# Which slots of an interleaved attention and MoE kernel run the first projection, in which PSUM bank, and which engine rectifies it

## The chip, the cores and the metric

The kernel runs on one core of a Trainium2 chip. The metric is the device time of one execution in microseconds. The engines are TensorE (PE in the profile, PEld for its weight loads), VectorE (DVE), ScalarE (ACT), GpSimd (POOL) and SyncE (SP, which here only issues DMAs).

## The reference

```python
# q, k, v: (8, 8, 576, 64) float32; w_in: (512, 2048); w_out: (2048, 512); tau = 0.02
scores = scale * np.matmul(q, k.transpose(0, 1, 3, 2))
thresh = np.max(scores, axis=-1, keepdims=True) - tau
scores = np.where(scores >= thresh, scores, -1000000000.0)
attn = np.exp(scores - np.max(scores, axis=-1, keepdims=True))
attn = attn / (np.sum(attn, axis=-1, keepdims=True) + 1e-09)
x = np.matmul(attn, v)             # heads side by side: (4608, 512)
h = x @ w_in
out = (h * np.clip(h + 3.0, 0.0, 6.0) / 6.0) @ w_out
```

So 64 heads of thresholded attention over 576 positions are followed by a two-layer MLP with a gated activation (the MoE part, with one expert). Below, "first projection" is the product with `w_in` and "second projection" the product with `w_out`.

## The kernel before

**Slots.** The order of all instructions is written out by hand; each engine runs its own instructions in that order and waits on semaphores. The work is cut into 144 slots, numbered n. A quad is four heads (two pairs) and takes nine slots: four for each pair, of 128 query rows of both heads, and one, slot 8 of the quad, for the last 64 rows of all four. Two quads make one batch element, so the order repeats with a period of 18 slots. I write c = n mod 18 for the place in the period.

**What one slot does, in the order of issue (the main loop, from L477).**

1. ScalarE: exponentials of the slot before with their sums (`sm_exp`, L309).
2. VectorE: two copies of the scores out of PSUM with row maxima (`sm_max`, L296); GpSimd makes a bias of each (L299).
3. One item of the first projection, if there is one to do: eight matmuls on TensorE (`mm1`, L372), a rectifier (`mm1_relu`: `r = max(h + 3, 0)`, on ScalarE at L380 or on VectorE at L382) and a gate on VectorE (`mm1_gate`, L387: `min(r, 6) * h`). In slots with an attention product the gate is put behind that product's copies.
4. VectorE: reciprocal of the sums of the slot before (`sm_recip`, L312).
5. In even slots only: up to two parts of the second projection (`mm2_part`, L397, four matmuls each; four parts make one output tile), and after a fourth part the output copy (`mm2_out`, L405 on VectorE), whose DMA is issued a slot later (L418).
6. ScalarE: masks (`sm_mask`, L304), which wait for the bias.
7. The slot's planned jobs: transposes of k on TensorE (L217, the 64 last rows L238) with a copy on ScalarE (L207), transposes of q (on VectorE, L226, from the third batch element on), attention products with v on TensorE (L341, L344) with copies on VectorE to `xT` (L352) and for the last rows to `xR` (L362).
8. After odd slots: scores of the two next slots on TensorE (L269, L275 for slot 8 of a quad). The scores of a slot need its PSUM region free, so the copies with maxima of the slot two before must have run.
9. GpSimd: normalisation of the slot before (`sm_norm`, L317); SP issues its DMA transposition (L325). GpSimd also issues the loads of v (L125, L129; one each in four slots of a period, c = 9 to 12) and at the start those of the weights (L146, L150).

From n = 22 (N1) on, attention products and transposes use PSUM banks 5 and 2, which the scores of even slots also use.

**Items.** The attention product at c = 3 (`av1`, with the rest `avr`) completes a batch element and puts 16 items into `todo1`. They run one a slot from c = 4 on. After the 8th and the 16th, eight parts of the second projection each go into `todo2`. Four batch elements' last rows make eight more items, `todo3`, which are there from n = 75 on and run only where `todo1` is empty. Attention products stand at c = 3, 9, 13 and 17.

**Banks.** A first projection accumulates in bank HB = 6; in odd slots it takes bank OB = 7, which is the second projection's, when `todo2` is empty:

```python
if todo1 or todo3:
    item, then = (todo1 or todo3).pop(0)
    h = mm1(item, hb=HB if n % 2 == 0 or todo2 else OB)
    r = mm1_relu(h, on_act=n % 2 == 0)
```

A projection can start in a bank only when the gate (or the output copy) that read the bank's last content is done.

Of the kernel before, what the change touches and what calls it, by code (L numbers as in the profile page):

```python
# [21 lines left out]
def kernel(  # L22
# [18 lines left out]
    NSLOT = 9  # L41
    NB = 2
    N1 = 22
    HB = 6
    OB = 7
# [74 lines left out]
    def load_v(b):  # L120
        vm = v_pool.tile([P, H, 4 * D], BF16, tag="vm", name="vm")
        vr = vrs[b % 2]
        vsb[b] = (vm, vr)
        for g in range(2):
            vcasts.append(lambda g=g: nc.gpsimd.dma_start(  # L125
                out=vm[:, g * 4:g * 4 + 4, :],
                in_=v[b, g * 4:g * 4 + 4, 0:512, :].rearrange("h (p t) d -> p h (t d)", t=4)))
        for a in range(2):
            vcasts.append(lambda a=a: nc.gpsimd.dma_start(  # L129
                out=vr[a * 64:(a + 1) * 64, a, :, :],  # L130
                in_=v[b, :, 512:S, :].rearrange("(hp a) p d -> a p hp d", a=2)[a]))
# [49 lines left out]
    def alloc_qk(quad):  # L181
        qkT[quad] = (qk_pool.tile([P, 2, S], F32, tag="qT", name="qT"),
                     qk_pool.tile([P, 2, S + 64], F32, tag="kT", name="kT"))
# [105 lines left out]
    def sm_max(sl):  # L289
        sl.s = s_pool.tile([P, 2, S], F32, tag="s", name="s")  # L290
        sl.m = stat_pool.tile([P, 2], F32, tag="m", name="m")
        sl.bias = stat_pool.tile([P, 2], F32, tag="bias", name="bias")
        sl.rsum = stat_pool.tile([P, 2], F32, tag="rsum", name="rsum")
        sl.rinv = stat_pool.tile([P, 2], F32, tag="rinv", name="rinv")
        for i in range(2):
            nc.vector.tensor_scalar(out=sl.s[:, i, :], in0=score_tile(sl.n, i),  # L296
                                    scalar1=1.0, scalar2=None, op0=Alu.mult, op1=Alu.max,
                                    accum_out=sl.m[:, i:i + 1])
            nc.gpsimd.tensor_scalar(out=sl.bias[:, i:i + 1], in0=sl.m[:, i:i + 1], scalar1=-scale, scalar2=tau,  # L299
                                    op0=Alu.mult, op1=Alu.add)  # L300

    def sm_mask(sl, i):
        s = sl.s[:, i, :]
        nc.scalar.activation(out=s, in_=s, func=Act.Prelu, bias=sl.bias[:, i:i + 1], scale=scale,  # L304
                             alpha=REJECT)

    def sm_exp(sl, i):
        s = sl.s[:, i, :]
        nc.scalar.activation(out=s, in_=s, func=Act.Exp, accum_out=sl.rsum[:, i:i + 1])  # L309

    def sm_recip(sl):
        nc.vector.reciprocal(out=sl.rinv[:], in_=sl.rsum[:])  # L312
# [15 lines left out]
    def pe_transpose(sl):  # L328
        pb = ps_flat[:, 3072:3072 + S].bitcast(BF16).rearrange("p (c t) -> p c t", t=P)
        pn = sl.pn[:].rearrange("p a b -> p (a b)")  # L330
        for c in range(9):
            nc.tensor.transpose(pb[:, c, :], pn[:, c * P:(c + 1) * P], identb[:])
        return lambda: nc.vector.tensor_copy(out=sl.dst, in_=pb)
# [33 lines left out]
    def mm1(item, hb=HB):  # L367
        src, ni, c0, _ = item
        hps = ps[:, hb, :].rearrange("p (n w) -> p n w", n=2)
        for n in range(2):  # L370
            for ki in range(KI):
                nc.tensor.matmul(hps[:, n, :], w_in_sb[:, ki, (ni + n) * P:(ni + n + 1) * P],  # L372
                                 src[:, ki, c0:c0 + 256], start=(ki == 0), stop=(ki == KI - 1))
        return hps


    def mm1_relu(hps, on_act):
        r = r_pool.tile([P, 2, 256], F32, tag="r", name="r")[:]
        if on_act:
            nc.scalar.activation(out=r, in_=hps, func=Act.Relu, bias=three[:])  # L380
        else:
            nc.vector.tensor_scalar(out=r, in0=hps, scalar1=3.0, scalar2=0.0, op0=Alu.add, op1=Alu.max)  # L382
        return r

    def mm1_gate(item, hps, r):
        _, ni, _, g0 = item
        nc.vector.scalar_tensor_tensor(out=gbuf[:, ni:ni + 2, g0:g0 + 256], in0=r, scalar=6.0, in1=hps,  # L387
                                       op0=Alu.min, op1=Alu.mult)
# [3 lines left out]
    def mm2_part(b, t, part, ob=OB):  # L392
        g0 = M + 64 * (3 - b % 4) if t == 4 else 512 * (b % 2) + P * t
        if part == 0:
            o_ps[0] = ps[:, ob, :]
        for ni in range(part * 4, part * 4 + 4):
            nc.tensor.matmul(o_ps[0], gbuf[:, ni, g0:g0 + P], w_out_sb[:, ni, :],  # L397
                             start=(ni == 0), stop=(ni == NI - 1))
# [12 lines left out]
    todo1 = []  # L411
    todo3 = []
    todo2 = []
# [63 lines left out]
    for n, sl in enumerate(queue):  # L477
        quad, slot = sl.quad, sl.slot
        b, g = divmod(quad, 2)
        now = n  # L480
        if slot in (0, 4):
            pts[2 * quad + slot // 4] = pt_pool.tile([P, 9, 512], BF16, tag="pT", name="pT")
        if slot == 8:
            ptr[quad] = ptr_pool.tile([P, 9, P], BF16, tag="pR", name="pR")
        if quad == 0 and slot == 0:
            load_quad(1)
        if slot == (4 if quad else 8) and quad + 2 < NQUAD:
            load_quad(quad + 2)
        if slot == 0 and g == 1 and b + 1 < B:
            load_v(b + 1)  # L490
        if prev is not None:
            for i in range(2):
                sm_exp(prev, i)
        sm_max(sl)

        gate = None
        if todo1 or todo3:
            item, then = (todo1 or todo3).pop(0)
            h = mm1(item, hb=HB if n % 2 == 0 or todo2 else OB)
            r = mm1_relu(h, on_act=n % 2 == 0)  # L500
            gate = lambda item=item, h=h, r=r: mm1_gate(item, h, r)
            if not any(job[:2] == "av" for job in plan[n]):
                gate()
                gate = None
            late2 = then
        else:
            late2 = ()
        copies = pe_transpose(queue[n - 2]) if n > 1 and queue[n - 2].on_chip else None
        if prev is not None:
            sm_recip(prev)  # L510
        if copies:
            copies()
        outs = []


        for _ in range(0 if n % 2 else 2):
            if todo2:
                b2, t2, part = todo2.pop(0)
                mm2_part(b2, t2, part)
                if part == 3:  # L520
                    outs += mm2_out(b2, t2, on_act=False)
        for i in range(2):
            sm_mask(sl, i)
        nxt = 2 * quad + 2
        for job in plan[n]:
            if gate and job[:2] != "av":
                gate()
                gate = None
            if job == "alloc":
                alloc_qk(quad + 1)  # L530
            elif job == "q1":
                transpose_q(2 * quad + 1)()
            elif job == "k1":
                transpose_k(2 * quad + 1)()
            elif job == "q0":
                transpose_q(nxt)()
            elif job == "k0":
                transpose_k(nxt)()
            elif job == "rest":
                transpose_rest(quad + 1)()  # L540
            elif job == "rest0":
                transpose_rest(0, of_k=False)()
            elif job == "av1":
                av_main(2 * quad - 1)
            elif job == "av0":
                av_main(2 * quad)
            elif job == "av0late":
                av_main(2 * quad - 2)
            elif job == "avr":
                av_rest(quad - 1)  # L550
                if quad % 2 == 0:
                    todo1.extend(moe_of(quad // 2 - 1))
                if quad % 8 == 0:
                    todo3.extend(moe_of_rest(quad // 2 - 1))
        if gate:
            gate()
        todo2.extend(late2)
        if n == 0:
            warm_up(8)
        if n <= N1:  # L560
            scores(n + 1)
        elif n % 2 and n + 2 < len(queue):
            scores(n + 1, n + 2)
        if n < 8:
            warm_up(6)
        if prev is not None:
            sm_norm(prev)
        flush()
        late.extend(outs)
        start(loads, 1)  # L570
        if n < 4 or n > 12:
            start(vcasts, 1)
        if n > 3:
            start(casts, 1 if n < 24 else 2)
        prev = sl
# [80 lines left out]
```

## Time and profile before

| | us |
|---|---|
| median of 6 runs | 577.79 |
| lowest and highest | 576.71 and 579.32 |
| the profiled execution | 578.01 |
| its span, first to last instruction | 576.2 |
| busy: PE, ACT, DVE, POOL | 533.6, 473.6, 424.9, 306.6 |
| mean granted TensorE clock | 0.994 |

The span is the time from the first to the last instruction of the profiled execution; some 1.8 us of its own time lie around it. A busy TensorE is not TensorE at its peak, since matmuls overlap in their pipeline and their ends are modelled. Slot 22 begins at 75.7 us and the last pair of slots (142 and 143) at 502.4 us; after it comes a tail with the last items.

### The profile page before, as it was taken

What the parts mean: (1) busy time and instruction counts of PE and PEld (TensorE: products, weight loads), DVE (VectorE), ACT (ScalarE), POOL (GpSimd) and SP (SyncE); (2) the same over time, 40 slices, a digit from 0 to 9 for tenths busy, and PEclk for the clock granted to TensorE, in tenths of its full rate; (3) what the DMA queues carried; (4) which work ended last, traced back from release to release, by engine and by line L of the source; (5) the groups of instructions that cost most, each with busy time, mean ns of one, the idle gap of its engine ahead of it and who ended that gap; (6) DMA issues with size and microseconds to landing.
All of it is one profiled execution on the core that took longest, in us unless ns stands there. A gap on an engine that the chain in (4) does not pass through costs nothing.

```text
span 576.2 us, 11988 instructions
## 1 busy us (share of the span) xinstructions
PE 533.6 (93%) x3998; PEld 327.8 (57%) x3998; DVE 424.9 (74%) x1060; ACT 473.6 (82%) x1012; POOL 306.6 (53%) x646
## 2 busy tenths in 40 slices
PE   8898888899989998999999998999989998989997
PEld 6654455555555565555555665556555565545853
DVE  3787876787888878787878888788878888751731
ACT  4899887899988899899989898989889899851730
POOL 2789867855565655655665556555565555530000
PEclk9998998999999999999999999999999999999999
DMA  5999979998698869986898779995898645562012
GB/s 116 140 137 180 176 119 188 167 166 157 134 164 142 145 152 150 154 160 120 160 172 146 140 128 152 149 163 108 161 160 147 139 99 104 83 118 74 1 37 73
DMA packets 286350, 77.54 MB, mean 135 GB/s; under 512 B 269264, under 2 KB 281808, under 8 KB 286288
## 3 DMA queue, kind: packets, MB, share of 16 engines
q1 hardware_dynamic: 267680, 67.47, 65.3%
q0 software_dynamic: 17408, 8.92, 13.5%
q8 instruction: 31, 0.51, 0.4%
q10 hardware_dynamic: 1200, 0.39, 0.3%
q14 instruction: 31, 0.25, 0.2%
HBM read 36.70 MB, written 9.44 MB: 80 GB/s over the span
## 4 chain that ended last, share of the span: by engine, by line
PE 50%; ACT 16%; DVE 10%; issue 5%; POOL 4%; DMA 2%; SPq 0%; POOLq 0%; DVEq 0%
PE ps L372 15%; PE ps L269 14%; PE ps L397 14%; ACT s L304 6%; DVE s L296 6%; ACT s L309 5%; PE ps L341 4%; ACT r L380 3%; POOL pn L317 3%; PE ps L275 2%; DMA w_out_sb<-in_moe_w_out_dram 1%; DVE g L387 1%; DVE osb L405 1%; PE ps L344 1%; ACT kT L207 1%
## 5 line engine op out<-in xcount | busy, mean ns | idle before, releaser
L317 POOL TENSOR_SCALAR pn<-s,rinv 128x576 bf16<-128x576 f32 x288 | 212.4, 748 | 106.6 <-DVE rinv L312 50.2
L296 DVE TENSOR_SCALAR_CACHE_REDUCE s<-ps 128x576 f32<-128x576 f32 x288 | 205.8, 752 | 54.7 <-PE ps L269 36.8
L304 ACT ACTIVATE s<-s,bias 128x576 f32<-128x576 f32 x288 | 206.4, 765 | 23.6 <-POOL bias L299 23.2
L309 ACT ACTIVATE s<-s 128x576 f32<-128x576 f32 x288 | 192.7, 671 | 0.3
L269 PE MATMUL ps<-kT,qT 64*128 64x192 f32 (+1 forms) x1024 | 167.7, 427 | 13.7 <-DVE s L296 9.1
L372 PEld LDWEIGHTS <-w_in_sb 128*128 128x128 bf16 x1152 | 107.6, 98 | 67.2 <-issue 51.7
L372 PE MATMUL ps<-xT,w_in_sb 128*128 128x256 bf16 x1024 | 130.5, 273 | 13.8 <-DVE osb L405 9.4
L397 PE MATMUL ps<-w_out_sb,g 128*128 128x512 bf16 x576 | 133.3, 379 | 0.8 <-ACT osb L403 0.7
L269 PEld LDWEIGHTS ps<-kT,qT 64*128 64x128 f32 x1024 | 95.5, 187 | 56.5 <-DVE s L296 24.0
L387 DVE SCALAR_TENSOR_TENSOR g<-r,ps 128x512 bf16<-128x512 f32 x144 | 98.6, 686 | 31.9 <-ACT r L380 30.4
L299 POOL TENSOR_SCALAR bias<-m 128x1 f32<-128x1 f32 x288 | 54.9, 191 | 97.1 <-DVE s L296 79.1
L397 PEld LDWEIGHTS <-g 128*128 128x128 bf16 x576 | 56.0, 98 | 59.5 <-issue 3.0
L380 ACT ACTIVATE r<-ps,three 128x512 f32<-128x512 f32 x86 | 58.7, 685 | 31.7 <-PE ps L372 31.2
L309 ACT ACTIVATION_READ_ACCUMULATOR s<-s 128x1 f32 x288 | 54.2, 188 | 0.0
L405 DVE TENSOR_SCALAR osb<-ps 128x512 f32<-128x512 f32 x30 | 20.6, 688 | 31.1 <-PE ps L397 31.1
L382 DVE TENSOR_SCALAR r<-ps 128x512 f32<-128x512 f32 x58 | 39.8, 686 | 0.6 <-PE ps L372 0.6
L341 PE MATMUL ps<-pT,vm 128*64 128x512 bf16 x256 | 33.7, 385 | 1.3 <-DMA pT<-pn 1.3
L312 DVE RECIPROCAL rinv<-rsum 128x2 f32<-128x2 f32 x144 | 23.0, 160 | 13.5 <-ACT s L309 13.3
L341 PEld LDWEIGHTS <-vm 128*64 128x64 bf16 x512 | 18.8, 110 | 18.0 <-issue 8.1
L207 ACT COPY kT<-ps 64x128 f32<-64x128 f32 (+1 forms) x55 | 22.8, 414 | 6.5 <-PE ps L217 3.5
L275 PE MATMUL ps<-kT,qT 64*64 64x384 f32 (+1 forms) x256 | 24.2, 431 | 3.2 <-DVE s L296 1.1
L403 ACT ACTIVATE osb<-ps 128x512 f32<-128x512 f32 x5 | 3.0, 597 | 28.9 <-PE ps L397 22.6
(43 smaller groups left out, 279.7 us busy)
## 6 DMA issues: line engine op xcount, KB each, us to landing
km<-in_k_dram SPq DMA_DIRECT2D x64, 128.0 KB, 3.1
out_dram<-osb SPq DMA_DIRECT2D x31, 256.0 KB, 2.5
nq<-in_q_dram SPq DMA_DIRECT2D x96, 72.0 KB, 3.0
vm<-in_v_dram POOLq DMA_DIRECT2D x16, 256.0 KB, 5.8
w_in_sb<-in_moe_w_in_dram POOLq DMA_DIRECT2D x16, 128.0 KB, 3.7
w_out_sb<-in_moe_w_out_dram POOLq DMA_DIRECT2D x16, 128.0 KB, 4.6
pT<-pn SPq DMA_TRANSPOSE x119, 3.6
nq<-in_q_dram SPq DMA_DIRECT2D x14, 128.0 KB, 4.2
```

Source lines behind the costliest of these rows:

```text
L269: nc.tensor.matmul(score_tile(n, a, k0=k0, w=w), qT_of(pair)[a * 64:(a + 1) * 64, t * P:(t + 1) * P], keys(pair, a, k0, w), start=True, st ...
L296: nc.vector.tensor_scalar(out=sl.s[:, i, :], in0=score_tile(sl.n, i), scalar1=1.0, scalar2=None, op0=Alu.mult, op1=Alu.max, accum_out=sl.m ...
L299: nc.gpsimd.tensor_scalar(out=sl.bias[:, i:i + 1], in0=sl.m[:, i:i + 1], scalar1=-scale, scalar2=tau, op0=Alu.mult, op1=Alu.add)
L304: nc.scalar.activation(out=s, in_=s, func=Act.Prelu, bias=sl.bias[:, i:i + 1], scale=scale, alpha=REJECT)
L309: nc.scalar.activation(out=s, in_=s, func=Act.Exp, accum_out=sl.rsum[:, i:i + 1])
L317: nc.gpsimd.tensor_scalar(out=pn[:, i, :], in0=sl.s[:, i, :], scalar1=sl.rinv[:, i:i + 1], scalar2=1.0, op0=Alu.mult, op1=Alu.mult)
L341: nc.tensor.matmul(pb[a * 64:(a + 1) * 64, :], vm[:, 2 * hp + a, c * D:(c + 1) * D], pT[:, 5 * a + c, cols], start=(c == 0), stop=False)
L372: nc.tensor.matmul(hps[:, n, :], w_in_sb[:, ki, (ni + n) * P:(ni + n + 1) * P], src[:, ki, c0:c0 + 256], start=(ki == 0), stop=(ki == KI - 1))
L380: nc.scalar.activation(out=r, in_=hps, func=Act.Relu, bias=three[:])
L382: nc.vector.tensor_scalar(out=r, in0=hps, scalar1=3.0, scalar2=0.0, op0=Alu.add, op1=Alu.max)
L387: nc.vector.scalar_tensor_tensor(out=gbuf[:, ni:ni + 2, g0:g0 + 256], in0=r, scalar=6.0, in1=hps, op0=Alu.min, op1=Alu.mult)
L397: nc.tensor.matmul(o_ps[0], gbuf[:, ni, g0:g0 + P], w_out_sb[:, ni, :], start=(ni == 0), stop=(ni == NI - 1))
```

## The change

Three things change in the loop. At c = 13 and c = 17, two of the four slots with an attention product, no item of `todo1` runs any more; an item of `todo3` runs there if there is one, and otherwise no first projection at all. Bank 7 is taken in an odd slot only when the even slot before it ran no part of the second projection (`parts` counts them). And at c = 4, 10 and 14 the rectifier goes to VectorE, where all odd slots have it.

```diff
@@ -494,17 +494,18 @@
         gate = None
-        if todo1 or todo3:
-            item, then = (todo1 or todo3).pop(0)
-            h = mm1(item, hb=HB if n % 2 == 0 or todo2 else OB)
-            r = mm1_relu(h, on_act=n % 2 == 0)
+        cyc = n % (2 * NSLOT)
+        if cyc in (13, 17) and not todo3 or not (todo1 or todo3):
+            late2 = ()
+        else:
+            item, then = (todo3 if cyc in (13, 17) or not todo1 else todo1).pop(0)
+            h = mm1(item, hb=HB if n % 2 == 0 or parts else OB)
+            r = mm1_relu(h, on_act=n % 2 == 0 and cyc not in (4, 10, 14))
             gate = lambda item=item, h=h, r=r: mm1_gate(item, h, r)
             if not any(job[:2] == "av" for job in plan[n]):
                 gate()
                 gate = None
             late2 = then
-        else:
-            late2 = ()
@@ -513,8 +514,11 @@
+        if n % 2 == 0:
+            parts = 0
         for _ in range(0 if n % 2 else 2):
             if todo2:
+                parts += 1
                 b2, t2, part = todo2.pop(0)
```

What a period holds, as the two programs' orders show it (R is an item of `todo3`; "out" is an output copy):

| c | jobs of the slot | before: bank, rectifier; second projection | after |
|---|---|---|---|
| 0 | | 6, ACT; 2 parts, out | 6, ACT; 2 parts, out |
| 1 | q | 7, DVE | 6, DVE |
| 2 | k | none, or R in 6, ACT; 2 parts | 6, ACT; none |
| 3 | products with rest | none, or R in 6, DVE | 7, DVE |
| 4 | k | 6, ACT; 2 parts, out | 6, DVE; 2 parts |
| 5 | q | 6, DVE | 6, DVE |
| 6 | rest of k | 6, ACT; 2 parts | 6, ACT; 2 parts, out |
| 7 | | 6, DVE | 6, DVE |
| 8 | | 6, ACT; 2 parts, out | 6, ACT; 2 parts |
| 9 | product, q | 7, DVE | 6, DVE |
| 10 | k | 6, ACT; none | 6, DVE; 2 parts, out |
| 11 | | 7, DVE | 6, DVE |
| 12 | | 6, ACT; 2 parts | 6, ACT; 2 parts |
| 13 | products with rest | 6, DVE | none, or R in 6, DVE |
| 14 | k | 6, ACT; 2 parts, out | 6, DVE; 2 parts, out |
| 15 | q | 6, DVE | 6, DVE |
| 16 | rest of k | 6, ACT; 2 parts | 6, ACT; 2 parts |
| 17 | product | 6, DVE | none, or R in 6, DVE |

Items of `todo3` ran at c = 2 and 3 in the three periods from n = 90 on before, and run at c = 13 and 17 in the four periods from n = 72 on after. So slots 31, 35, 49, 53, 67 and 71 have no first projection after the change. Four items of the first projection and 18 parts of the second are left for the tail in both. In all, 18 rectifiers move from ScalarE to VectorE.

## The prediction

> **What bounds the kernel now.** I read the page first.
>
> ```profile
> PE 533.6 (93%) x3998; PEld 327.8 (57%) x3998; DVE 424.9 (74%) x1060; ACT 473.6 (82%) x1012; POOL 306.6 (53%) x646
> ```
>
> No engine is full, so the answer lies in who waits for whom. The waits list next (engine, line, whom it waited for: us in total, times, longest):
>
> ```profile
> DVE g L387 <- ACT r L380: 30.4, 82, 1.8
> PE ps L372 <- DVE osb L405: 9.4, 12, 0.8
> PE ps L372 <- DVE g L387: 4.4, 6, 1.1
> ```
>
> TensorE's first projection waits 12 times for an output copy to empty bank 7, and 6 times for a gate to empty bank 6. Then the timeline, cut by the start of the first row-maximum copy (L296) of each slot. The pairs repeat to about 0.01 us from one period to the next, so I cut one period (191.33 to 254.15 us, c = 0 to 17) into its nine pairs of slots. Columns: stretch, its length, busy time by engine.
>
> ```profile
> 191.33:198.06 6.73, 5.95 (x40) 3.70 (x38) 6.28 (x15) 6.09 (x14) 2.75 (x7) 1.00 0.84 156
> 198.06:204.67 6.61, 6.51 (x61) 3.60 (x61) 3.82 (x14) 5.80 (x14) 4.68 (x10) 1.00 0.88 145
> 204.67:211.40 6.73, 6.50 (x44) 4.17 (x42) 6.28 (x16) 6.27 (x13) 2.76 (x7) 1.00 0.50 94
> 211.40:217.99 6.59, 6.59 (x52) 4.02 (x52) 4.91 (x14) 6.25 (x16) 4.21 (x10) 1.00 0.82 172
> 217.99:225.83 7.84, 7.06 (x52) 4.06 (x51) 6.80 (x16) 7.31 (x17) 4.93 (x10) 1.00 0.89 144
> 225.83:231.62 5.79, 4.96 (x36) 3.31 (x34) 4.91 (x13) 4.46 (x9) 3.26 (x8) 1.00 1.22 189
> 231.62:239.91 8.29, 7.71 (x73) 4.74 (x73) 5.76 (x15) 7.54 (x18) 6.07 (x12) 1.00 1.10 152
> 239.91:247.12 7.21, 6.92 (x54) 4.05 (x53) 6.29 (x16) 6.77 (x15) 3.23 (x8) 1.00 0.71 140
> 247.12:254.15 7.03, 7.03 (x53) 4.22 (x52) 5.50 (x15) 6.54 (x16) 4.21 (x9) 1.00 0.89 143
> ```
>
> The pairs run from 5.79 to 8.29 us: the work is uneven. In 16-17 TensorE is busy throughout; in 0-1 and 4-5 VectorE's order sets the length. The longest, 12-13, follows from a chain that its rows show:
>
> ```profile
> 229.89 0.80 POOL L125 DMA_DIRECT2D vm<-in_v_dram  x1
> 230.77 0.46 POOL L299 TENSOR_SCALAR bias<-m 128x1 f32<-128x1 f32 x2
> 230.98 1.44 ACT L304 ACTIVATE s<-s,bias 128x576 f32<-128x576 f32 x2 [0.43 <-POOL bias L299]
> 234.36 0.69 DVE L387 SCALAR_TENSOR_TENSOR g<-r,ps 128x512 bf16<-128x512 f32 x1 [1.29 <-ACT r L380]
> 235.10 1.03 PE L372 MATMUL ps<-xT,w_in_sb 128*128 128x256 bf16 x8 [0.58 <-DVE g L387]
> ```
>
> GpSimd issues a V load before the bias of slot 11; ScalarE's masks, exponentials and then slot 12's rectifier come late; the gate follows 2.74 us after 231.62 instead of the usual 1.61; slot 13's projection waits in bank 6.
>
> **The change part by part.** Durations are distances between starts (the next instruction starts before the last has drained). VectorE: both maxima 1.35 (207.90 to 209.25), rectifier, gate, reciprocal from
>
> ```profile
> 209.25 0.69 DVE L382 TENSOR_SCALAR r<-ps 128x512 f32<-128x512 f32 x1
> 209.97 0.69 DVE L387 SCALAR_TENSOR_TENSOR g<-r,ps 128x512 bf16<-128x512 f32 x1
> 210.57 0.16 DVE L312 RECIPROCAL rinv<-rsum 128x2 f32<-128x2 f32 x1
> ```
>
> 0.72, 0.60, 0.08; output copy 0.61 (207.29 to 207.90). TensorE: a first projection 0.88 before a second one and 0.97 elsewhere, two parts of the second 1.72, transposes of k 0.43, an attention product 1.20, with the rest's 1.52; from the scores' start to the next maximum 2.34 (251.81 to 254.15). An odd slot without attention product takes 3.50 from its maximum to the next (207.90 to 211.40), 3.98 where slot 8 of a quad is scored (243.14 to 247.12): scores wait for its maxima. These stay.
>
> Periods 2 to 7 hold most of it. The first projections' last two move to c=2 and 3, so second projections move from c=2,4,6,8 to 4,6,8,10, and output copies from 4 and 8 to 6 and 10.
>
> *Pair 4-5, six times.* Slot 4 loses the output copy and rectifies on VectorE: 1.35+0.72+0.60+0.08 = 2.75 against 3.23 (204.67 to 207.90). Slot 5's projection needs bank 6 at 2.75+0.05; TensorE arrives at 2.85 (207.52): no wait. 2.75+3.50 = 6.25: -0.48.
> *Pair 6-7, six times.* Slot 6 gains the output copy, which waits for the second projection's end at 2.89 (214.29-211.40): 2.93+0.61 = 3.54, +3.98 = 7.52 against 6.59: +0.93.
> *Pair 8-9, six times.* Without the copy slot 8 lasts 2.29, as slot 16 does (247.12 to 249.41); its gate ends at 2.30, so bank 6 is free before TensorE is: -0.21+0.88+1.73 = 2.40. Then 0.97+1.20+2.34: 6.90 (6.91, rounding) against 7.84: -0.94. The 0.78 waits for bank 7 go.
> *Pair 10-11, six times.* VectorE's rectifier and the copy: 2.75+0.61 = 3.36, +3.49 = 6.85 against 5.79: +1.06.
> These four: +0.57 a period, +3.42.
>
> *Pair 2-3.* Both projections, no second one, in all periods. ScalarE: the rectifier at 1.21 (324.90-323.69, in a period that has it there today), masks 1.79, kT copy 3.12, exponentials 3.60; then, with the distances of
>
> ```profile
> 202.62 0.17 DVE L312 RECIPROCAL rinv<-rsum 128x2 f32<-128x2 f32 x1 [1.70 <-ACT s L309]
> 203.29 0.28 DVE L362 CAST xR<-ps 128x128 bf16<-128x128 f32 x1
> 204.67 0.76 DVE L296 TENSOR_SCALAR_CACHE_REDUCE s<-ps 128x576 f32<-128x576 f32 x1 [1.09 <-PE ps L269]
> ```
>
> reciprocal 5.07 (1.47 after the exponentials' start, 201.15 to 202.62), xR copy 5.74, next maximum 1.38 later: 7.12. Periods 2 to 4 had no projection there: 6.61, +0.51 three times; 5 to 7 had two and a second projection: 7.98, -0.86 three times. Sum -1.05.
>
> *Pair 12-13.* Slot 11's maximum comes 1.06 later, GpSimd's norm and V load only 0.45 (its norm starts behind reciprocal 10, the one issued in slot 10, now at 2.67 instead of 2.22). So slot 11's bias starts at 5.40 after slot 10's maximum, masks 0.21 later, exponentials 1.34 and their end 1.33 after that (230.98, 232.33, 233.66): 8.28, which is 1.43 into slot 12. The rectifier starts there, the gate at 2.12: -0.62. Periods 4 to 7 still project in slot 13 (the remainder's items): -0.62 twice, -1.04 at 422.83 (8.71 before, where a V load was late; to 7.67), -0.20 at 487.44 (7.75, without V loads). Periods 2 and 3 skip it: TensorE would be ready at 6.6, but exponentials (3.31), reciprocal (4.78), xR copy (5.45), then 1.38 give 6.83: -1.46 twice. Sum -5.40.
>
> *Pair 14-15, six times:* VectorE's rectifier ends behind the second projection: 2.75+0.61 against 3.23: +0.13, +0.78. *Pair 16-17* without slot 17's projection (periods 1 to 3): exponentials, reciprocal at 4.82 and xT copy end at 5.58, +1.10 = 6.68 against 7.03: -0.35 three times, -1.05. *Pair 0-1:* slot 1's projection starts 0.85 earlier in bank 6, but the scores wait for VectorE: nothing. Period 1 else: 0.4 gained before slot 14 meets the wait for w_out's landing (second projection to 116.87) there. The tail holds four first and eighteen second parts either way: nothing. Output DMAs follow their copies two slots later on SP's queue, past loads and transpositions; at about 0.5 us of queue each (osb's median issue is 528 ns) they could hold up a transposition of pn by that much, and its product comes slots later: nothing.
>
> Sum: 3.42-1.05-5.40+0.78-1.05 = -3.30. Profiled execution 578.01 (span 576.2): 574.7; against the median 577.79: 574.5.
>
> The trace has no VectorE rectifier in an even slot. Bounds: nothing (masks and exponentials start earlier and return it) to 0.72 each; slots 4, 10, 14 carry 0.46, 0.46, 0.13 here, 6.3 in all, so -9.6 to +3.4; I take the VectorE distance, its nearest row.
>
> Two rules speak against the change. Rows: rectifiers last 685 ns on ScalarE and 686 on VectorE, but the next starts 0.59 (205.56 to 206.15) and 0.72 later. The Trainium skill (Perfetto Trace Analysis, Optimizing Scalar/DVE Operations) gives PSUM access about 125 ns on VectorE and 51 on ScalarE; an estimate with the clocks of 0.96 and 1.2 GHz that VectorE: DVE Perf Modes and ScalarE: Activation LUTs state under Specifications is 0.66 against 0.48 for 512 elements: 18 moved ones would give back 3.2 us of the 3.3. And rows: bank 7 costs waits of 0.78 at slots 1 and 9, bank 6 one of 0.58 at 13; at slot 11, which moves from a free bank 7 to bank 6, TensorE comes at 2.85 behind a gate that ends at 2.75, and the scores behind wait for VectorE. The same page (Optimizing Tensor Performance, Matmuls) wants independent groups to rotate through PSUM banks. By it slot 11 would lose something like the 0.58, six times: an estimate of 3.5 us, and no change.
>
> **The rivals.** *The attention slots give little:* if GpSimd's V load and norm slide the full 1.06 with slot 11, slot 12 stays at 3.42: the four 12-13 terms of periods 4 to 7 vanish (+2.48) and the two skips lose 0.62 each (+1.24): 574.5+3.7 = 578.2, no change. For it: GpSimd queues all biases behind loads. Against: its norm waits for reciprocal 10, not for slot 11.
> *Slower:* the pairs that should shorten are already TensorE's. With both projections, 4-5 needs 0.89+1.73+0.43+0.97+2.34 = 6.36 less the 0.20 head start, 6.16: only 0.09 of room under 6.25. If TensorE's shadows (weight loads, hidden waits in the scores) keep 4-5 at 6.73 and 8-9 gains only the 0.66 by which the gate frees bank 6 before the copy frees bank 7 (220.62, 221.28), so 7.18, that costs 6x0.48+6x0.28 = 4.6: 579.1. It decides from 0.75 a period: 4.5 turns -3.3 into +1.2. Against: 16-17 shows those groups back to back in 7.03.
> *A larger gain:* VectorE's rectifiers free ScalarE and cost nothing in 14 and half in 4 and 10: -0.8-2.8, 570.9.
>
> **How the numbers follow.** A measurement of this kernel can tell about 0.2% (1.2 us) from no change. Forecast 0.63, larger gain 0.11: together faster by over 0.2%, 0.74. No change 0.12, slower 0.14. The range runs from 571.5, near the larger gain, to 578.3, just past the no-change case; the slower case and half of the gain's tail stay out. The faster case alone: 572 to 576.5.
>
> **What would show it.** After: no wait of L372 for L405, pairs 4-5 near 6.25, 8-9 near 6.9, 12-13 at 7.7 and 6.8, against 6-7 at 7.5 and 10-11 at 6.85; 18 rectifiers fewer on ScalarE. Wrong: slot 12's gate still 2.7 after its maximum; VectorE idle in slot 4 or 10; 2-3 above 7.3.

## The result, and the profile after

| | before | after |
|---|---|---|
| median, us | 578.43 (46 runs) | 576.3 (20 runs) |
| lowest and highest, us | 575.71 and 581.09 | 573.89 and 577.7 |
| the profiled execution, us | 578.01 | 576.54 |
| its span, us | 576.2 | 574.6 |
| slots 36 to 142 of it, us | 373.87 | 372.13 |
| busy PE, ACT, DVE, us | 533.6, 473.6, 424.9 | 537.2, 463.3, 435.2 |

The ratio of after to before is 0.9954 [0.9943, 0.9965]: faster by 0.46%, some 2.7 us, where the forecast had 0.57%. The two medians of the table are only 2.1 us apart, and the two profiled executions 1.5 us. The 576.3 us lie inside the range of 571.5 to 578.3.

The page of the changed kernel:

```profile
PE 537.2 (93%) x3998; PEld 329.0 (57%) x3998; DVE 435.2 (76%) x1078; ACT 463.3 (81%) x994; POOL 306.6 (53%) x646
```

ScalarE has 18 instructions fewer and VectorE 18 more. Its groups of instructions (busy us, mean ns of one, idle time before):

```profile
L382 DVE TENSOR_SCALAR r<-ps 128x512 f32<-128x512 f32 x76 | 52.1, 686 | 0.0
```

That was x58 before. The count is a net one: three rectifiers a period move at c = 4, 10 and 14, in seven periods, which is 21, while at c = 2 six projections now rectify on ScalarE where three did before. Its list of waits:

```profile
DVE g L387 <- ACT r L380: 23.1, 60, 1.9
PE ps L372 <- DVE g L387: 1.0, 3, 0.6
```

The line of L372 waiting for the output copy L405 (9.4 us, 12 times) is gone altogether, and the waits of L372 for a gate fell from 4.4 us to 1.0. The windows of the changed kernel, cut as before by the first row maximum of each slot, show the same period (c = 0 to 17 from 190.77 us), and as a tenth row a pair 12-13 that runs a last-rows item in slot 13 (columns: stretch, its length, busy time of PE, PEld, DVE, ACT, POOL, clock, DMA share, GB/s):

```profile
190.77:198.02 7.25, 6.58 (x42) 3.89 (x40) 6.29 (x16) 6.97 (x16) 3.23 (x8) 1.00 0.87 162
198.02:205.13 7.11, 6.72 (x69) 4.34 (x69) 5.69 (x17) 6.37 (x15) 4.68 (x10) 1.00 0.97 162
205.13:211.38 6.25, 6.25 (x44) 4.17 (x42) 6.18 (x15) 5.23 (x12) 2.75 (x7) 1.00 0.34 65
211.38:218.92 7.54, 6.95 (x52) 4.04 (x52) 5.62 (x15) 7.49 (x19) 4.21 (x10) 1.00 1.06 157
218.92:225.82 6.90, 6.90 (x52) 4.07 (x51) 6.24 (x15) 6.16 (x14) 4.88 (x10) 1.00 0.86 175
225.82:232.68 6.86, 6.50 (x44) 4.18 (x42) 6.12 (x16) 5.00 (x11) 3.53 (x9) 1.00 1.14 167
232.68:239.43 6.75, 6.75 (x65) 3.89 (x65) 4.50 (x14) 6.00 (x14) 5.38 (x12) 1.00 1.34 152
239.43:246.75 7.32, 6.91 (x54) 4.05 (x53) 6.78 (x17) 7.04 (x17) 3.71 (x9) 1.00 0.96 165
246.75:252.90 6.15, 6.15 (x43) 3.55 (x41) 4.30 (x12) 5.54 (x14) 3.73 (x9) 1.00 0.89 166
294.81:302.40 7.59, 7.59 (x73) 4.75 (x73) 5.75 (x16) 6.84 (x17) 5.85 (x12) 1.00 1.09 192
```

The pairs ran from 5.79 to 8.29 us before; in these windows they now run from 6.15 to 7.59. The reader should see three things. The pairs 4-5 (6.25), 6-7 (7.54), 8-9 (6.90) and 10-11 (6.86) stand where the forecast put them (6.25, 7.52, 6.90, 6.85). In 4-5, 8-9, 12-13 and 16-17 TensorE's busy time now equals the length, which alone does not make TensorE the limit: e1 below does the same work of 4-5 in 6.16. And 0-1, which was to stay at 6.73, takes 7.25, while 16-17 takes 6.15 where 6.68 was forecast.

### The profile page after: what moved, and what is told of

Same layout as the page of the kernel before. It is cut to its first block, busy times and chain, and to the rows that moved or that the text cites. A ratio compares the mean times of both kernels' runs of the same rounds, so it can differ in the third digit from the quotient of the medians.

```text
span 574.6 us, 11939 instructions
## 1 busy us (share of the span) xinstructions
PE 537.2 (93%) x3998; PEld 329.0 (57%) x3998; DVE 435.2 (76%) x1078; ACT 463.3 (81%) x994; POOL 306.6 (53%) x646
## 4 chain that ended last, share of the span: by engine, by line
PE 57%; DVE 16%; ACT 8%; issue 3%; DMA 2%; POOL 2%; DVEq 0%; POOLq 0%
PE ps L269 19%; PE ps L397 16%; PE ps L372 14%; DVE s L296 10%; PE ps L341 4%; ACT s L304 3%; PE ps L275 3%; ACT s L309 2%; DVE r L382 2%; DMA w_out_sb<-in_moe_w_out_dram 2%; DVE osb L405 1%; ACT r L380 1%; DVE g L387 1%; POOL pn L317 1%; PE ps L344 1%
## 5 line engine op out<-in xcount | busy, mean ns | idle before, releaser
L296 DVE TENSOR_SCALAR_CACHE_REDUCE s<-ps 128x576 f32<-128x576 f32 x288 | 205.8, 752 | 50.6 <-PE ps L269 32.7
L269 PE MATMUL ps<-kT,qT 64*128 64x192 f32 (+1 forms) x1024 | 173.1, 429 | 19.4 <-DVE s L296 12.6
L372 PEld LDWEIGHTS <-w_in_sb 128*128 128x128 bf16 x1152 | 107.5, 98 | 52.4 <-issue 36.3
L372 PE MATMUL ps<-xT,w_in_sb 128*128 128x256 bf16 x1024 | 130.2, 273 | 0.4 <-DVE g L387 0.4
L380 ACT ACTIVATE r<-ps,three 128x512 f32<-128x512 f32 x68 | 46.3, 683 | 21.0 <-PE ps L372 20.3
L382 DVE TENSOR_SCALAR r<-ps 128x512 f32<-128x512 f32 x76 | 52.1, 686 | 0.0
L405 DVE TENSOR_SCALAR osb<-ps 128x512 f32<-128x512 f32 x30 | 20.5, 683 | 30.3 <-PE ps L397 24.1
```

The source lines that it names most:

```text
L269: nc.tensor.matmul(score_tile(n, a, k0=k0, w=w), qT_of(pair)[a * 64:(a + 1) * 64, t * P:(t + 1) * P], keys(pair, a, k0, w), start=True, st ...
```

## The experiments

Every kernel was timed beside runs of the kernel before on the same chip, and its ratio is to those. The traces give a sharper measure too. From the first maximum of slot 36 to that of slot 142 a kernel repeats from run to run to about 0.1 us: the changed kernel took 372.13 and 372.08 us there in two profiled executions, e1's kernel 367.91 and 367.94. I call this stretch the steady part; it is worked out from the starts of L296 in the timeline. Ahead of slot 36 two traces of one kernel differ by 1.45 to 2.41 us; behind the start of slot 142 all twelve traces take 73.8 to 73.9 us. This table says how many us the pairs of the steady part gained or lost against the kernel before, summed over the six periods (five for 16-17):

| pair | after | e1: all but rectifiers | e2: rectifiers alone | e3: bank rule alone | e4: skips alone |
|---|---|---|---|---|---|
| 0-1 | +1.54 | +1.19 | 0.00 | 0.00 | +1.20 |
| 2-3 | -0.74 | -1.11 | -0.02 | -0.02 | -1.11 |
| 4-5 | -2.85 | -3.45 | +0.73 | +0.01 | -3.45 |
| 6-7 | +5.67 | +4.57 | -0.01 | 0.00 | +4.57 |
| 8-9 | -5.65 | -5.65 | +0.36 | -4.00 | -5.65 |
| 10-11 | +6.39 | +5.66 | +2.80 | -0.01 | +5.67 |
| 12-13 | -5.07 | -5.81 | -0.72 | -0.02 | -5.81 |
| 14-15 | +0.72 | +0.04 | +0.73 | 0.00 | +0.03 |
| 16-17 | -1.75 | -1.40 | 0.00 | 0.00 | -1.39 |
| sum | -1.74 | -5.96 | +3.87 | -4.04 | -5.94 |

**e1: the three rectifiers back on ScalarE.** The changed kernel with one line altered:

```diff
-            r = mm1_relu(h, on_act=n % 2 == 0 and cyc not in (4, 10, 14))
+            r = mm1_relu(h, on_act=n % 2 == 0)
```

> The changed kernel with the rectifiers of c = 4, 10 and 14 back on ScalarE. Theory A (the chains of the prediction): the move costs VectorE's order 0.46 us in slot 4 and 0.13 in slots 10 and 14, and ScalarE has room, because its kT copies wait for TensorE in these slots. Slot 4 then lasts 2.29 us, pair 4-5 is TensorE's at 5.85 instead of 6.26, pair 6-7 gives 0.17 back (7.7, slot 6's rectifier behind slot 5's exponentials), 10-11 lasts 6.72 and 14-15 7.2: about 3 us less than the changed kernel, 573 us or a ratio of 0.990 to the kernel before. Rival B (ScalarE, busy 82% before, needs the relief): the rectifier again delays masks and kT copies by 0.59 us in three slots of six periods, up to 10 us more than the changed kernel; a ratio of 1.00 or more.

Measured: 570.78 us against 578.0, ratio 0.9873 [0.9852, 0.9895]. The windows of 4-5, 6-7 and 10-11:

```profile
204.45:210.61 6.16, 6.16 (x46) 4.07 (x45) 5.67 (x14) 5.70 (x12) 2.81 (x7) 1.00 0.40 76
210.61:217.97 7.36, 6.80 (x51) 3.85 (x50) 5.51 (x15) 7.31 (x19) 4.13 (x10) 1.00 1.07 152
224.87:231.60 6.73, 6.50 (x44) 4.17 (x42) 5.61 (x15) 5.80 (x13) 3.50 (x9) 1.00 1.18 148
```

The moved rectifiers cost the change 4.22 us of the steady part (-5.96 against -1.74), more than the 3 expected; that the relief of ScalarE would be worth something falls. Where the cost sits was missed: 5.85 was expected of 4-5, but it takes 6.16 with TensorE busy through all of it, so only 0.10 of a possible 0.46 is saved there. But 6-7 gains 0.18 as well, since TensorE enters slot 6 with a head start (its first projection starts 0.19 before the slot's maximum, and 0.12 after it in the changed kernel).

**e2: the rectifiers alone.** The kernel before with one line altered:

```diff
-            r = mm1_relu(h, on_act=n % 2 == 0)
+            r = mm1_relu(h, on_act=n % 2 == 0 and n % (2 * NSLOT) not in (4, 10, 14))
```

> The kernel before with only the three rectifiers of c = 4, 10 and 14 on VectorE. Theory A: slot 10 goes from 2.29 to 2.75 us, slots 4 and 14 from 3.23 to 3.36: 0.72 a period, six periods, less some 0.4 in the first one: 4 us slower, ratio 1.007. Rival B (the relief of ScalarE is what gains): 1 to 3 us faster, ratio 0.995 to 0.998.

Measured: 581.26 us against 578.0, ratio 1.0056 [1.0037, 1.0075]: slower. The window of 10-11:

```profile
225.22:231.47 6.25, 4.95 (x36) 3.31 (x34) 5.51 (x14) 4.00 (x9) 3.35 (x8) 1.00 1.24 166
```

It took 5.79 before. The 0.46 of slot 10 is here in full (TensorE has room, 4.95 of 6.25), 4-5 and 14-15 lose 0.12 each, and 12-13 wins 0.12 a period back on average. The +0.36 of 8-9 in the table is a single pair (slots 80 and 81), for which the profile names no cause. ScalarE did become freer, and it brought nothing that outweighs this.

**e3: the bank rule alone.** The kernel before with the new condition:

```diff
-            h = mm1(item, hb=HB if n % 2 == 0 or todo2 else OB)
+            h = mm1(item, hb=HB if n % 2 == 0 or parts else OB)
...
+        if n % 2 == 0:
+            parts = 0
...
+                parts += 1
```

> The kernel before with only the bank rule of the change. It moves the projections of c = 1 and c = 9 from bank 7 to bank 6. Theory A: slot 9's projection starts when slot 8's gate ends instead of when the output copy does, 0.66 us earlier, and pair 8-9 falls from 7.84 to about 7.23 (then VectorE's order ends last); slot 1 gains nothing, since its scores wait for VectorE: 3.7 us faster, ratio 0.9937. Rival C (projections that share a bank wait for each other's gates, so that turns between banks are needed): the two waits of 0.78 become waits for the gate of about the same length; ratio 1.000 or above.

Measured: 573.88 us against 578.0, ratio 0.9925 [0.9907, 0.9943]: by itself it gains more than the whole change (in the steady part 4.04 us against 1.74). Its window of 8-9:

```profile
216.60:223.78 7.18, 7.07 (x52) 4.09 (x51) 6.68 (x17) 6.98 (x16) 4.40 (x10) 1.00 0.94 139
```

7.84 became 7.18, which is the 0.66 by which the gate frees bank 6 before the output copy frees bank 7. Pair 0-1 stays at 6.73: the wait of 0.78 at slot 1 went too, and cost nothing. So the rival by which the projections must alternate banks falls.

**e4: the skips alone.** The kernel before with the new choice of items, the old bank rule and the rectifiers on ScalarE:

```diff
-        if todo1 or todo3:
-            item, then = (todo1 or todo3).pop(0)
+        cyc = n % (2 * NSLOT)
+        if cyc in (13, 17) and not todo3 or not (todo1 or todo3):
+            late2 = ()
+        else:
+            item, then = (todo3 if cyc in (13, 17) or not todo1 else todo1).pop(0)
             h = mm1(item, hb=HB if n % 2 == 0 or todo2 else OB)
             r = mm1_relu(h, on_act=n % 2 == 0)
```

> The kernel before with only the two skipped slots (and with them the shift of the last projections, second projections and output copies); rectifiers and bank rule as before. Theory A: with the shifted second projections the old rule already keeps slot 9 in bank 6; it puts slots 1 and 11 in bank 7, where they wait for the output copy, but the scores behind wait longer for VectorE. So the same as with the new bank rule: equal to the run that differs from the changed kernel by the rectifiers alone, to within 0.5 us, ratio 0.990. Rival D (the bank wait is on the path at slots 1 and 11): 0.8 us in two slots of six periods, up to 9 us more than that run, ratio up to 1.005.

Measured: 571.16 us against 578.0, ratio 0.9886 [0.9865, 0.9908]. Its steady part, 367.93 us, is that of e1 (367.91) pair by pair. Its list of waits:

```profile
PE ps L372 <- DVE osb L405: 6.8, 12, 0.8
```

The waits for bank 7 are still there, twelve of them, six of 0.78 at c = 1 and six of 0.35 at c = 11, and they cost nothing, since the pairs take as long without them in e1. Alone the skips gain 5.94 and the bank rule 4.04, together 5.96: the gains don't add. Both remove the same wait at slot 9, the bank rule by name, the skips because they shift the second projections so that the old rule keeps slot 9 in bank 6 too.

**after_again and e5: the wait for w_out.** In the changed kernel's profiled execution the pair 14-15 of the first period with projections took 8.89 us, against 7.44 before (a window, then two rows of its timeline):

```profile
113.59:122.48 8.89, 7.24 (x54) 4.05 (x53) 6.89 (x17) 6.50 (x16) 3.23 (x8) 1.00 1.12 169
```

```profile
116.77 0.38 PE L397 MATMUL ps<-w_out_sb,g 128*128 128x512 bf16 x1 [1.03 <-DMA w_out_sb<-in_moe_w_out_dram]
117.48 0.38 PE L397 MATMUL ps<-w_out_sb,g 128*128 128x512 bf16 x1 [0.33 <-DMA w_out_sb<-in_moe_w_out_dram]
```

The second projection of slot 32 waits 1.36 us for its weights. The changed kernel was therefore run once more, beside a version of it that starts two weight loads a slot from slot 16 on instead of 24:

```diff
-            start(casts, 1 if n < 24 else 2)
+            start(casts, 1 if n < 16 else 2)
```

> The changed kernel once more, to have it on the same chip as the next two. Both theories: ratio 0.995 to the kernel before, pairs of slots as in its first trace to 0.02 us; what may differ is slot 32 (c = 14 of the first period with projections), which waits for the landing of w_out (4.91 us in the first trace, 3.35 in other periods), and slots 111 and 120, each 0.4 to 0.7 us longer there than in the other periods.

> The changed kernel with the weights' loads two a slot from slot 16 on instead of slot 24 (the last one in slot 25 instead of 29). Theory A: the wait in slot 32 (1.03 and 0.33 us for w_out's last two loads) goes, and slots 27 to 30 lose GpSimd's load issues, so the biases of slots 28 to 31 come earlier: 1.4 us from the wait and up to 1 us from the biases, less what two issues cost in slots 16 to 23: 1 to 2.5 us less than the changed kernel, ratio 0.991 to 0.993. Rival E (the wait is for DMA bandwidth, not for the issue): w_out lands as late as before and nothing is gained, ratio 0.995.

Measured: after_again 575.64 us against 578.83, ratio 0.9949 [0.9932, 0.9966]; e5 574.72, ratio 0.9935 [0.9917, 0.9953]. By time this is inconclusive, as the intervals overlap. The traces say why: this time the changed kernel itself had no wait in slot 32 (3.49 us for the slot, against 4.91 in the first trace), so there was little to remove; and in e5 slots 19 and 21, where the loads now lie, are longer by 0.8 and 0.7 us. So are slots 24 to 26, but there TensorE's granted clock stood at 0.5 for 6.83 us from 89.15 us on; in e6_again, with the same loads and the full clock, they are not. The part of rival E by which w_out lands as late as before falls: in e5 its last load lands at 97.15 us, in after_again at 115.64.

**e6: both, ScalarE's rectifiers and the early loads.** The edits of e1 and e5 together.

> Both: the rectifiers of c = 4, 10 and 14 back on ScalarE, and the weights' loads two a slot from slot 16 on. Theory A: the two gains add, since they lie in different slots: about 4 us from the rectifiers (0.9873 measured for them alone) and 1 to 2.5 from the loads: ratio 0.983 to 0.986, about 569 us. Rival E: as with the rectifiers alone, 0.987.

Measured: 568.74 us against 578.83, ratio 0.9828 [0.981, 0.9846]: the lowest ratio of all runs, faster than both kernels. To see what the early loads bring beside e1's edit, e1 and e6 were repeated together, with a version of e1 that moves the loads the other way:

```diff
-            start(casts, 1 if n < 24 else 2)
+            start(casts, 1 if n < 26 else 2)
```

> The changed kernel with the three rectifiers on ScalarE, once more, beside the next two on one chip. Theory A: ratio 0.987 to 0.989; slot 32 waits 0 to 1.8 us for w_out.

> The same with the weights' loads two a slot from slot 16 on. Theory A: slot 36 starts 1.5 to 2 us earlier (126.6 against 128.5 in the first traces) and nothing changes behind it: 1.5 to 2 us less, ratio 0.983 to 0.985. Rival E: what the loads cost in slots 19 to 26 eats it, same time as the run beside it within 0.5 us.

> The same with the weights' loads two a slot only from slot 26 on, so the last one in slot 30 instead of 29, one slot later and behind one more V load. Theory A: the landing of w_out ends last in slot 32, and slot 36 starts 2.5 to 4 us later (a slot's length, less room where there was no wait): ratio 0.992 to 0.995. Rival E (the landing is set by bandwidth, or the wait is an accident of one run): no change, 0.988.

Measured, against 577.66: e1_again 571.0, ratio 0.9892 [0.9871, 0.9912]; e6_again 569.53, ratio 0.9853 [0.9834, 0.9872]; e7_late 575.2, ratio 0.9951 [0.9933, 0.9968]. The same row of slot 32 in the three timelines, e1_again first, then e7_late, then e6_again:

```profile
117.61 0.76 PE L397 MATMUL ps<-w_out_sb,g 128*128 128x512 bf16 x2 [2.20 <-DMA w_out_sb<-in_moe_w_out_dram]
```

```profile
119.41 0.96 PE L397 MATMUL ps<-w_out_sb,g 128*128 128x512 bf16 x2 [2.07 <-DMA w_out_sb<-in_moe_w_out_dram]
```

```profile
111.40 1.89 PE L397 MATMUL ps<-w_out_sb,g 128*128 128x512 bf16 x8
```

Later loads make slot 32 wait more (7.34 us for the slot in e7_late, with 3.3 us of waits in three pieces; 5.75 in e1_again), earlier ones take the wait away. Slot 36 starts at 131.51 us in e7_late, 129.97 in e1_again and 124.16 in e6_again. The steady parts do not differ (367.92 to 367.94), so what separates these kernels lies ahead of slot 36. That the landing of w_out ends last in slot 32 stands for e1_again and e7_late, and the rival in which the wait is only an accident of one run falls: with the loads issued later the time rose by 4.2 us. How much the early loads are worth is less sharp: the intervals of e1_again and e6_again just touch, and e6's slot 36 lies at 126.57 and 124.16 against 128.52 and 129.97 in e1, of which the half-clock stretches told of below take a part (e6_again has none, the others two or three).

## Why the prediction was right, step by step

**The direction, and the kernel as it stood:** right. The wait of L372 for L405 is gone, 12-13 is no longer 8.29 (but for the pair at slot 120), and the early pairs are where they were put: 4-5, 6-7, 8-9 and 10-11 to 0.02 us, 14-15 at 7.32 against 7.34, 2-3 at 7.11 against 7.12.

**Pair 12-13:** right, and its chain can be read off the changed kernel's timeline (slot 10's maximum is at 225.82, slot 12's at 232.68):

```profile
230.25 0.80 POOL L125 DMA_DIRECT2D vm<-in_v_dram  x1
231.12 0.46 POOL L299 TENSOR_SCALAR bias<-m 128x1 f32<-128x1 f32 x2
231.34 1.44 ACT L304 ACTIVATE s<-s,bias 128x576 f32<-128x576 f32 x2 [0.54 <-POOL bias L299]
234.72 0.69 DVE L387 SCALAR_TENSOR_TENSOR g<-r,ps 128x512 bf16<-128x512 f32 x1 [0.60 <-ACT r L380]
```

The bias of slot 11 comes 5.30 after slot 10's maximum (5.40 forecast) and slot 12's gate 2.04 after its own (2.12 forecast, 2.74 before). GpSimd's V load came 0.37 later against slot 10 (4.06 to 4.43), not the 1.06 by which slot 11 slid, so the rival in which the attention slots give little falls. The pairs take 7.59 and 6.75, a little under 7.67 and 6.83. One did not follow: the pair at slot 120 took 8.30, +0.63, behind a V load that GpSimd issued late,

```profile
420.11 0.81 POOL L125 DMA_DIRECT2D vm<-in_v_dram  x1 [0.36 <-issue]
```

for a reason the profile does not name ("issue"). The forecast had taken the lateness of the same load before (8.71) for an accident that would go. It is none: this load has 0.35 to 0.37 us of such idle time ahead of it in all twelve traces, whatever the kernel. In the three traces of the changed order with its rectifiers on VectorE, GpSimd's norm ahead of it starts 0.3 later too.

**Pairs 16-17 and 0-1:** the sum was right, the place wrong. 16-17 without a projection was to wait 1.10 from the end of the xT copy and 0-1 to stay: 6.68 + 6.73 = 13.41. Measured is 6.15 + 7.25, which is 13.40. Slot 0's maximum follows earlier, and the delay of ScalarE's chain shows a slot later:

```profile
252.90 0.76 DVE L296 TENSOR_SCALAR_CACHE_REDUCE s<-ps 128x576 f32<-128x576 f32 x1 [0.57 <-PE ps L269]
255.03 0.69 DVE L387 SCALAR_TENSOR_TENSOR g<-r,ps 128x512 bf16<-128x512 f32 x1 [0.68 <-ACT r L380]
```

The gate of slot 0 waits 0.68 for a rectifier that ScalarE does behind slot 17's exponentials. The forecast's 1.10 from the end of a copy to the next maximum is the one of slot 3 (203.57 to 204.67), where the copy of the rest comes last. In slot 17 the xT copy ends 5.58 after slot 16's maximum, as forecast, but the next maximum follows 0.57 later. It comes 2.33 after the scores' start at 250.57, which is the prediction's 2.34 for TensorE. That the sum of the two pairs still came out to 0.01 is luck, since nothing in the forecast ties the one error to the other.

**The rectifiers:** the kind of cost was right, its size between the bounds. They were put at 0.46, 0.46 and 0.13 in slots 4, 10 and 14, 6.3 in six periods; they cost 4.22 inside the change and 3.87 alone. Slot 4 did grow by the 0.47 (2.76 against 2.29 in e1), but e1's slot 5 gives 0.36 of it back, since TensorE sets the pair. In slot 10, where the change also puts the output copy, only 0.12 is lost; the 0.46 appears there in e2, without the copy. The rival of a larger gain, in which the rectifiers cost little, falls: the larger gain is that of the change without them (e1, 0.9873).

**The slower rival** had the right limit but not the decisive one: 6.16 for 4-5, which it worked out as TensorE's own time, is what e1 shows to the hundredth. The changed kernel's VectorE stays 0.09 above it, as the prediction said, and 8-9 gained its full 0.94.

**The two rules.** That rectifiers are dearer on VectorE was the one to heed: 4.22 us over the 18 moved ones of the steady part is 0.23 each. The two distances of the rows differ by only 0.13 (0.72 against 0.59); the rest comes from the place in the order, as slot 4 shows, which grew by 0.47. The estimate from the Trainium skill (Perfetto Trace Analysis, Optimizing Scalar/DVE Operations) had 3.2 in all; the runs agree with its direction and are somewhat above it, but they do not test its two figures, since the cost is not the difference of the two engines alone. That matmul groups should rotate through PSUM banks (the same page, Optimizing Tensor Performance, Matmuls) the runs speak against here: the second bank is another product's, and staying out of it gained 4.04 us in e3. The loss that the prediction worked out from this rule for c = 11, 3.5 us, did not come: no projection at c = 11 waits for a gate in the changed kernel (the three waits left are in slots 113, 121 and 140).

**What was mis-sized.** In the two profiled executions slot 142 begins 1.63 us earlier (502.39 to 500.76), against the 3.3 of the sum. Three terms together miss 2.0. The pair at slot 120 misses 0.63. Slot 111 misses 0.37: it took 4.87 instead of 4.50 us, in all three traces of the changed order with this placement of the rectifiers and in none with them on ScalarE. The maximum behind it waits for something that the profile puts down to scores which had long ended, so the cause stays open. The step "period 1 else: nothing" misses 1.0. The other pairs 12-13, 0.08 shorter than forecast in four periods, give 0.3 back, which leaves the missing 1.7. Of the 1.0: the 0.4 gained in period 1 did meet the wait for w_out's landing, as the prediction said, but the last load landed a further 1.0 later than before (117.44 against 116.45 us), and 14-15 rose by 1.45, from 7.44 to 8.89. The second trace of the same kernel has no such wait, so this term varies from run to run. It is not shown to be an accident, though: of the five traces that skip slot 31's projection and keep the loads where they were, four have the wait (slot 32 takes 4.91 to 5.92 us there), and of the three that project in slot 31 (before, e2, e3) none has more than 0.33 us of it.

**How much of the agreement is luck.** The steady part's -1.7 (-1.8 in the second trace of the changed kernel) is what the change surely brings. The rest of the measured 2.7 must lie ahead of slot 36, if the other runs are like the traces, since all of these take the same time behind slot 142. The first traces of the two kernels have the same two half-clock stretches there and reach slot 36 at 128.52 and 128.63, so they show no gain there; the second trace of the changed kernel has one stretch and no wait, and reaches it at 126.83. How much of that rest is the change's is not settled. So the chains of the prediction are borne out pair by pair, but that 2.7 came so close to 3.3 is in part luck.

Not tried: V loads in other slots of the period, which slot 120 calls for, and either of the two skipped slots without the other.

## What to carry to other kernels

Take a change that does three things apart before believing its sum: here two parts gained 4.0 and 5.9 us alone, 6.0 together because both removed one wait, and the third gave 4.2 back. The busy shares (ScalarE 82%, VectorE 74%) suggested moving work from the one to the other; the order in which the maximum, rectifier, gate and copy stand on VectorE ahead of the next scores said the opposite and was right. And a wait in the list, like the twelve of 0.78 us for bank 7, is worth only what the work behind it was not already waiting for: half of them were worth 0.66 each, and half nothing.

## What the runs showed of the hardware

The first 130 us vary by 1.45 to 2.41 us between two traces of one kernel; the 370 us behind them repeat to 0.1. One reason is the landing of w_out's loads: up to 8.5, 10.6 and 10.5 us from load to landing in the traces of before, after and e1_again, and at most 5.7 where they were issued earlier. Another is the granted clock. The page's slices of it for the changed kernel (tenths of full speed, 14.4 us each) and for e6_again:

```profile
PEclk9998998999999999999999999999999999999999
```

```profile
PEclk9999999999999999999999999999999999999999
```

The two 8s, about 54 and 88 us after the start, are stretches of 3.41 us in which the clock stood at 0.5. The second trace of the changed kernel has only the second of them. e1_again has one at about 119 us, right behind its wait of 2.20 us for w_out, in which slot 33 took 4.80 us instead of 3.98. The two other traces with a wait of 2.0 us there, e4 and e7_late, have one at the same place, and no other trace has: in after and e1 the longest wait is 1.03 and none follows. From 135 us on all kernels here ran at 1.0 until the last two microseconds. What brings such a stretch on is not shown beyond that.
